# How 128 half rows of a weight matrix are dealt out to partitions: two loads or nine

## The chip, the cores and the metric

The kernel runs on one NeuronCore of a Trainium2 chip. The metric is the device time of one execution in microseconds. Three executions of the kernel before took 400.17, 400.23 and 400.68 us; the median is 400.23.

## The reference

One token is decoded. Its normalised row `xn` goes through an attention block over a cache of 65,536 keys and through a small mixer with two matrix pairs; both results are added to the input.

```python
xn = _layernorm(x)                                  # x: 1 x 1 x 1024, bfloat16
# A: 32 query heads, 4 key heads, 65536 keys of 128
q = xn @ wq                                         # 1024 x 4096
p = softmax(q . k_cache / sqrt(128))
A = (p @ v_cache) @ wo                              # 4096 x 1024
# B: 1024 -> 1024 -> 1024, then 1024 -> 3584 -> 1024
h = gelu(layernorm(xn) @ w1)
g0..g3 = the four quarters of h, each shifted along the sequence, zeros coming in
hs = concatenate([g0, g1, g2, g3]) @ w2
x1 = xn + hs
B = x1 + gelu(layernorm(x1) @ w3) @ w4
return x + A + B
```

The sequence has one position, so every shift brings in zeros only: `hs` is zero for any w2. The kernel still reads w2 and multiplies it, by a column of zeros (`g_col`). Therefore any placement of w2's values in the on-chip memory gives the same output, as long as all of w2 is loaded.

The inputs are 64 MB of keys, 64 MB of values, wq and wo of 8 MB each, w3 and w4 of 7 MB each, w1 and w2 of 2 MB each.

## The kernel before

All large inputs are streamed through three buffers of the on-chip memory, `slots`, of 128 partitions times 64 KB. The list `stream` (L298) holds their order: wq, w3, w1 and w2 together (`w12`), then for each of 8 units `u` a K block and a V block of 8 MB, then wo, then w4. Item number i uses buffer i mod 3. `load` (L301) records the loads of an item, all on SyncE's queue (SP), and `freed` (L332) is called after the last reader of an item has been recorded: it loads the item three places later into the same buffer. The loads of one queue are issued in the order in which they were recorded.

The functions record operations into a `Program` (L59). `plan` (L134) then works out which operation must wait for which other, from the memory regions that they read and write (`regions`, L30, which takes a write to every fourth partition apart into single partitions). Each load gets a semaphore of its own (`landed_n`), which counts to 16 when the load is complete (L207-209). An operation with several waits gets all but the last as separate wait instructions ahead of it (L200-206).

w2 has 1024 rows of 1024 values. It is cut into 2048 half rows of 512 values (1 KB each; `HALF`, L25). The main load of w2 (L312) puts 15 consecutive half rows (`W2_RUN`) into each of the 128 partitions, 1920 in all. The other 128 half rows, 128 KB, go in extra loads, told by the list `W2_EXTRAS` (L27): before, 20 half rows to each of 5 partitions (0, 4, 8, 12, 16), then 14 to each of 2 partitions (1 and 5). They lie behind the 15 half rows of the main load, in columns that POOL sets to zero first (`pool.memset`, L362), since most partitions get nothing there. `W2_DEEP` (L262) is the number of half-row columns that the extras take up: 20.

`compute_w12` (L453) multiplies w1 (16 matmuls), and then adds w2 up in PSUM with one matmul for each column of half rows (L461-462): 15+20 = 35 matmuls. They read the columns of all partitions, so they wait for the extra loads too. Then the buffer is free, and the load of the second K block follows on SP.

For each unit, `scores` transposes K on VectorE (DVE) and multiplies it on TensorE (PE), `maxima` and `weights` make the softmax weights, `values` multiplies V. At the end come wo and w4; w4 is loaded in five pieces (`W4_PIECES`, L19) so that little work is left when the last has landed.

Of the kernel before, what the change touches and what calls it, by code (L numbers as in the profile page):

```python
# [14 lines left out]
P = 128  # L15
# [8 lines left out]
PITCH = {}  # L24
HALF = 512  # L25
W2_RUN = 15
W2_EXTRAS = ((0, 5, 20), (1, 2, 14))  # L27


def regions(ap):  # L30
# [186 lines left out]
def kernel(  # L217
# [15 lines left out]
    D = A_x.shape[-1]  # L233
# [17 lines left out]
    prog = Program(nc)  # L251
    pe, dve, act, pool = prog, prog.dve, prog.act, prog.pool

    def sb(name, shape, dtype=F32):
        return nc.alloc_sbuf_tensor(name, list(shape), dtype)
# [3 lines left out]

    slots = [sb(f"slot{i}", [P, ROW], BF16) for i in range(3)]  # L260
    PITCH.update({t[:].tensor.name: ROW * 2 for t in slots})
    W2_DEEP = max(m for _, _, m in W2_EXTRAS)  # L262
    assert sum(k * m for _, k, m in W2_EXTRAS) == D * D // HALF - P * W2_RUN
    p_sb = sb("p_sb", [P, SUBS * 512], BF16)
    og = sb("og", [P, 512])
    x_row = sb("x_row", [32, D], BF16)
# [34 lines left out]
    def load(it):  # L301
        t = tiles[it]
        if it == "wq":
            prog.load("sp", t[:], A_wq.rearrange("(p c) n -> p (c n)", c=DC))
        elif it == "w3":
            prog.load("sp", t[:, 0:DC * F], B_w3.rearrange("(p c) f -> p (c f)", c=DC))
        elif it == "w12":
            prog.load("sp", t[:, 0:DC * D], B_w1.rearrange("(p c) n -> p (c n)", c=DC))
            at = DC * D
            halves = B_w2.rearrange("r (h n) -> (r h) n", n=HALF)  # L310
            first = P * W2_RUN
            prog.load("sp", t[:, at:at + W2_RUN * HALF], halves[0:first, :].rearrange("(m c) n -> m (c n)", c=W2_RUN))  # L312
            at += W2_RUN * HALF
            for b, k, m in W2_EXTRAS:
                prog.load("sp", t[b:b + 4 * k - 3:4, at:at + m * HALF],
                          halves[first:first + k * m, :].rearrange("(q c) n -> q (c n)", c=m))
                first += k * m
        elif it == "wo":
            prog.load("sp", t[:], A_wo.rearrange("(p j) n -> p (j n)", p=P))
        elif it == "w4":  # L320
            w4_v = B_w4.rearrange("(m c) n -> m c n", c=FC)
            c0 = 0
            for n in W4_PIECES:
                prog.load("sp", t[:, c0 * D:(c0 + n) * D], w4_v[:, c0:c0 + n, :].rearrange("p c n -> p (c n)"))
                c0 += n
        else:
            kind, i = it
            g, b = divmod(i, NB)
            cache = A_k_cache if kind == "K" else A_v_cache
            prog.load("sp", t[:], cache[0, g, b * UKEYS:(b + 1) * UKEYS, :].rearrange("(p ct) d -> p (ct d)", p=P))  # L330

    def freed(it):  # L332

        n = stream.index(it) + 3
        if n < len(stream):
            load(stream[n])

    load("wq")
    opening = len(prog.ops)

    dve.memset(x_row[:], 0.0)
    prog.load("act", x_row[0:1, :], A_x[0, 0:1, :])
    load("w3")

    pool.memset(ident_f[:], 0.0)
# [14 lines left out]
    pool.memset(g_col[:], 0.0)  # L360
    w2_end = DC * D + (W2_RUN + W2_DEEP) * HALF
    pool.memset(tiles["w12"][:, w2_end - W2_DEEP * HALF:w2_end].bitcast(F32), 0.0)  # L362
    load("w12")

    def row_acc(j, lhsT, rhs, start=False):
        return pe.mm(psB[32 * j:32 * j + 32, :], lhsT.to_broadcast([P, 32]), rhs, start, False, (0, 32 * j), COLS)
# [7 lines left out]
    def layernorm(src, tag):  # L374
        rowsum = sb(f"ln_rowsum_{tag}", [P, 1])
        dve.reduce_sum(out=rowsum[:], in_=src[:], axis=AX.X)
        at = next_pm()
        pe.mm32(at[:, 0:1], ones_f[:], rowsum[:], True, True)
        negmean = sb(f"ln_negmean_{tag}", [P, 1])
        dve.tensor_scalar(out=negmean[:], in0=at[:, 0:1], scalar1=-1.0 / D, scalar2=None, op0=ALU.mult)  # L380
        cen = sb(f"ln_cen_{tag}", [P, DC])
        dve.tensor_scalar(out=cen[:], in0=src[:], scalar1=negmean[:, 0:1], scalar2=None, op0=ALU.add)
        sq = sb(f"ln_sq_{tag}", [P, DC])
        rowsq = sb(f"ln_rowsq_{tag}", [P, 1])
        dve.tensor_tensor_reduce(out=sq[:], in0=cen[:], in1=cen[:], scale=1.0, scalar=0.0,
                                 op0=ALU.mult, op1=ALU.add, accum_out=rowsq[:])
        pe.mm32(at[:, 1:2], ones_f[:], rowsq[:], True, True)
        std = sb(f"ln_std_{tag}", [P, 1])
        act.activation(out=std[:], in_=at[:, 1:2], func=ACTF.Sqrt, bias=eps_t[:, 0:1], scale=1.0 / D)
        rstd = sb(f"ln_rstd_{tag}", [P, 1])  # L390
        dve.reciprocal(out=rstd[:], in_=std[:])
        normed = sb(f"ln_out_{tag}", [P, DC])
        dve.tensor_scalar(out=normed[:], in0=cen[:], scalar1=rstd[:, 0:1], scalar2=None, op0=ALU.mult)
        rep = sb(f"ln_rep_{tag}", [P, DC, 32], BF16)
        dve.tensor_copy(out=rep[:], in_=normed[:].unsqueeze(2).to_broadcast([P, DC, 32]))
        return normed, rep, negmean, rstd

    xn, xn_rep, negmean1, rstd1 = layernorm(xT, "a")
    _, xn2_rep, _, _ = layernorm(xn, "b")
# [53 lines left out]
    def compute_w12():  # L453
# [6 lines left out]
        act.activation(out=h1, in_=sc[0:32, 0:2, :], func=ACTF.Gelu_apprx_tanh)  # L460
        for c in range(W2_RUN + W2_DEEP):  # L461
            row_acc(c % 2, g_col[:], wt[:, 2 * DC + c, :], start=(c < 2))
# [86 lines left out]
    for u in range(NU):  # L549
        g, b = divmod(u, NB)  # L550
# [88 lines left out]
```

## Time and profile before

| what | value |
|---|---|
| median of three runs | 400.23 us (400.17, 400.23, 400.68) |
| profiled execution, in all | 400.13 us |
| its span (first to last instruction) | 398.8 us |
| bytes loaded | 170.03 MB, 426 GB/s over the span |
| granted TensorE clock, mean | 0.795 |
| load of w3: issued, first used by PE | 2.30 us, 39.68 us |
| main load of w2 | 1920 KB, 47.2 us from issue to landing |
| K loads, V loads (8 of each) | median 42.2 and 36.8 us from issue to landing |
| last piece of w4 | 256 KB, 34.2 us from issue to landing |

The span is the time between the first and the last instruction on the core; 1.3 us of the 400.13 lie around it. A load's time from issue to landing includes the time in which it stands behind earlier loads, so 42 us for a K block doesn't mean that 8 MB take that long. Two views carry most here: the chain of waits, which is followed back from the last instruction to what released each step, and the DMA packets, of which the trace keeps start, duration, size and queue.

### The profile page before, as it was taken

To read this page: it belongs to the slowest core of one execution; us is meant where nothing else is said; L and a number is where in the kernel's file an instruction comes from. 1 tells how busy PE (TensorE), PEld (TensorE's weight loads), DVE (VectorE), ACT (ScalarE), POOL (GpSimd) and SP (SyncE) were. 2 spreads that over 40 slices of the span, in tenths; PEclk is the share of its full clock that TensorE was granted. 3 is DMA by queue.
4 is the path that set the end of the run, shared out by engine and by line. 5 is a ranking of instruction groups with operands and counts; after the bars stand their busy time and mean duration, and the time that the engine had idled before them with its cause. 6 is when DMAs were issued, how large, how long until landed. Compare 5 with 4: busy or idle time off the path is not lost.

```text
span 398.8 us, 2582 instructions
## 1 busy us (share of the span) xinstructions
PE 226.0 (57%) x1379; PEld 45.2 (11%) x890; DVE 210.2 (53%) x156; ACT 27.6 (7%) x35; POOL 10.6 (3%) x30
## 2 busy tenths in 40 slices
PE   0250990592469256923874197529552946393587
PEld 0210000010101020001001000201010102010233
DVE  0520010975096549653963795259439932793411
ACT  1010030002000200020002000200010011002000
POOL 7000000000000000000000000000000000000000
PEclk9996797597859666978796779568967995687669
DMA  8989999999999999999999999999999999999996
GB/s 342 493 375 419 470 427 421 435 460 434 429 421 434 427 435 434 440 440 434 416 434 440 434 421 442 440 427 427 427 449 440 421 434 435 427 427 421 409 438 274
DMA packets 3774, 170.03 MB, mean 426 GB/s; under 512 B 426, under 2 KB 428, under 8 KB 685
## 3 DMA queue, kind: packets, MB, share of 16 engines
q1 hardware_dynamic: 3758, 169.87, 98.8%
q8 instruction: 9, 0.15, 0.1%
q14 instruction: 1, 0.01, 0.0%
q10 hardware_dynamic: 6, 0.00, 0.0%
HBM read 169.87 MB, written 0.00 MB: 426 GB/s over the span
## 4 chain that ended last, share of the span: by engine, by line
DMA 62%; PE 20%; DVE 15%; ACT 2%; issue 0%; SPq 0%
DMA slot<-in_A_k_cache_dram 44%; DMA slot<-in_B_w_dram 18%; PE sc L116 14%; DVE slot L92 11%; PE oacc L116 4%; DVE p_sb L92 2%; DVE mx L92 2%; ACT p_sb L92 2%; PE psB L116 1%; PE pm L132 0%; DVE m L92 0%; DVE rep L92 0%; DVE nball L92 0%; DVE x_halves L92 0%; PE pm L116 0%
## 5 line engine op out<-in xcount | busy, mean ns | idle before, releaser
L116 PE MATMUL sc<-slot,qdiag 128*128 128x512 bf16 x512 | 130.9, 418 | 65.7 <-DVE slot L92 65.6
L92 DVE STREAM_TRANSPOSE slot<-slot 128x4096 f32<-128x4096 f32 x32 | 139.4, 4411 | 52.2 <-DMA slot<-in_A_k_cache_dram 52.2
L116 PE MATMUL oacc<-slot,p_sb 128*32 128x512 bf16 x512 | 44.5, 524 | 37.5 <-DVE p_sb L92 18.8
L92 DVE STREAM_TRANSPOSE p_sb<-p_sb 128x2048 bf16<-128x2048 bf16 (+2 forms) x10 | 20.8, 2085 | 38.7 <-ACT p_sb L92 38.5
L92 DVE TENSOR_REDUCE mx<-sc 128x1 f32<-128x2048 f32 x8 | 18.3, 2292 | 30.6 <-PE sc L116 30.6
L112 PEld LDWEIGHTS <-qdiag 128*128 128x128 bf16 x128 | 13.2, 103 | 181.4 <-issue 181.4
L92 ACT ACTIVATE p_sb<-sc,nball 128x2048 bf16<-128x2048 f32 x8 | 15.7, 1967 | 250.7 <-DVE nball L92 250.7
L112 PEld LDWEIGHTS <-p_sb 128*32 128x32 bf16 x512 | 16.3, 127 | 62.4 <-issue 19.8
L116 PE MATMUL sc<-slot,ln_rep_b 128*32 128x512 bf16 (+1 forms) x80 | 16.2, 828 | 9.1 <-DMA slot<-in_B_w_dram 8.9
L132 PE MATMUL pm<-ident_f,mx 128*1 128x128 f32 x8 | 2.2, 270 | 19.1 <-DVE mx L92 19.1
L92 DVE SCALAR_TENSOR_TENSOR og<-oacc,wb,og 128x512 f32<-128x512 f32 x4 | 3.0, 751 | 18.8 <-PE oacc L116 18.8
L92 POOL COPY qdiag<-qx 32x32 bf16<-32x32 bf16 x16 | 3.2, 203 | 272.5 <-PE sc L116 250.6
L116 PE MATMUL psB<-slot,oT 128*32 128x512 bf16 x64 | 9.2, 457 | 1.2 <-DVE oT L92 1.2
L126 PE MATMUL pm<-ol,selx 128*128 128x129 f32 x8 | 2.6, 415 | 10.6 <-DVE ol L92 10.6
L116 PE MATMUL sc<-slot,ln_rep_a 128*32 128x512 bf16 x64 | 5.7, 532 | 4.4 <-DMA slot<-in_A_wq_dram 4.4
L126 PE MATMUL pm<-ln_rowsum_a,msk 128*128 128x1 f32 x2 | 0.6, 362 | 13.3 <-DVE ln_rowsum_a L92 13.3
L92 DVE TENSOR_TENSOR og<-psB,slot 64x512 f32<-64x512 f32 x1 | 0.7, 683 | 13.1 <-PE psB L116 13.1
L92 DVE STREAM_TRANSPOSE p_sb<-x_row 32x256 bf16<-32x256 bf16 x4 | 2.5, 616 | 7.4 <-DMA x_row<-in_A_x_dram 7.4
L116 PE MATMUL psB<-slot,g_col 128*32 128x512 bf16 x35 | 4.9, 379 | 0.0
L132 PE MATMUL pm<-ident_f,rep 1*128 1x1 f32 x8 | 1.9, 234 | 5.0 <-DVE rep L92 5.0
L92 ACT COPY og<-oacc 128x512 f32<-128x512 f32 x4 | 2.3, 585 | 32.1 <-PE oacc L116 32.1
L116 PE MATMUL psB<-slot,hT 128*32 128x512 bf16 x40 | 4.5, 379 | 0.0
(87 smaller groups left out, 65.5 us busy)
## 6 DMA issues: line engine op xcount, KB each, us to landing
slot<-in_B_w_dram SPq DMA_DIRECT2D x1, 7168.0 KB, 37.3
slot<-in_B_w_dram SPq DMA_DIRECT2D x2, 2048.0 KB, 37.8
slot<-in_B_w_dram SPq DMA_DIRECT2D x1, 3072.0 KB, 33.4
slot<-in_B_w_dram SPq DMA_DIRECT2D x1, 1920.0 KB, 47.2
slot<-in_B_w_dram SPq DMA_DIRECT2D x1, 1280.0 KB, 33.2
slot<-in_B_w_dram SPq DMA_DIRECT2D x1, 512.0 KB, 34.1
slot<-in_B_w_dram SPq DMA_DIRECT2D x1, 256.0 KB, 34.2
slot<-in_A_k_cache_dram SPq DMA_DIRECT2D x8, 42.2
```

The costliest lines, as they stand in the source:

```text
L92: return program.add(Op(engine, lambda: method(*args, **kw), reads, writes, alone=kw.get("accum_out") is not None))
L112: self.add(Op("pe", lambda: pe.ldweights(lhsT, tile_position=pos), [lhsT], []))
L116: return pe.add_instruction(mybir.InstMatmult(name=nc.get_next_instruction_name(), engine=mybir.EngineType.PE, start_tensor_calc=start, st ...
L126: return self.add(Op("pe", lambda: pe.matmul(out, lhsT=lhsT, rhs=rhs, start=start, stop=stop, tile_position=pos, skip_group_check=True), [ ...
L132: return self.add(Op("pe", lambda: pe.transpose(out, in_, identity), [in_, identity], [out]))
```

## The change

The list of extra loads gets a fourth number, the column at which a load starts. The same 128 half rows are dealt out in nine loads: 12 half rows to each of 3 partitions (0, 4, 8); 1 to each of 8 partitions (1, 5, ... 29); and seven loads of one half row to each of 9, 10, 11, 12, 13, 14 and 15 partitions (32, 36, 40, ...), the load of k partitions in column k-9. The columns of the extras go from 20 to 12, and with them the memset on POOL (5120 to 3072 words a partition) and the matmuls over w2 (35 to 27). The order of the loads on SP stays: the nine stand where the two stood, behind the main load of w2 and ahead of the first K block.

```diff
-W2_EXTRAS = ((0, 5, 20), (1, 2, 14))
+W2_EXTRAS = ((0, 3, 12, 0), (1, 8, 1, 0)) + tuple((32, k, 1, k - 9) for k in range(9, 16))
...
-    W2_DEEP = max(m for _, _, m in W2_EXTRAS)
-    assert sum(k * m for _, k, m in W2_EXTRAS) == D * D // HALF - P * W2_RUN
+    W2_DEEP = max(m + c for _, _, m, c in W2_EXTRAS)
+    assert sum(k * m for _, k, m, _ in W2_EXTRAS) == D * D // HALF - P * W2_RUN
...
-            for b, k, m in W2_EXTRAS:
-                prog.load("sp", t[b:b + 4 * k - 3:4, at:at + m * HALF],
+            for b, k, m, c in W2_EXTRAS:
+                prog.load("sp", t[b:b + 4 * k - 3:4, at + c * HALF:at + (c + m) * HALF],
                           halves[first:first + k * m, :].rearrange("(q c) n -> q (c n)", c=m))
                 first += k * m
```

## The prediction

> **What bounds the kernel now.** I read the busy rows first, then the DMA rows by queue, then the chain of waits, and last the trace's packets one by one. The page's first two parts:
>
> ```profile
> PE 226.0 (57%) x1379; PEld 45.2 (11%) x890; DVE 210.2 (53%) x156; ACT 27.6 (7%) x35; POOL 10.6 (3%) x30
> ...
> DMA  8989999999999999999999999999999999999996
> GB/s 342 493 375 419 470 427 421 435 460 434 429 421 434 427 435 434 440 440 434 416 434 440 434 421 442 440 427 427 427 449 440 421 434 435 427 427 421 409 438 274
> ```
>
> No compute engine passes 57%, while the 16 DMA engines are at 80% or more in every slice but the last. The stream of bytes sets the time. The end of the chain of waits (start, duration, what) says the same:
>
> ```profile
> 362.56 34.22 DMA slot<-in_B_w_dram
> 396.79 0.04 issue
> 396.83 0.34 PE pm L116 x4
> 397.17 0.02 issue
> 397.19 0.43 DVE x_halves L92
> ```
>
> The last piece of w4 is issued at 362.56 and counted as landed at 396.79; 2.0 us of tail follow to 398.8. So the question is which of the 16 DMA engines finishes last. The DMA part by queue shows what runs beside the loads:
>
> ```profile
> q1 hardware_dynamic: 3758, 169.87, 98.8%
> q8 instruction: 9, 0.15, 0.1%
> q14 instruction: 1, 0.01, 0.0%
> ```
>
> Nine packets of 16 KB and one of 8 KB fetch instructions. The trace lists each DMA packet with start, duration and size. A packet of 64 KB takes 2.418 us and the next one of the same engine starts 3 to 4 ns before its end, so the packets can be strung into 16 streams. Each stream runs without a pause from 1.92 to 2.46 us until its end, except where an instruction fetch falls into it: then the next packet is late by 1.0 to 1.4 us. The streams, as I strung them (KB of the two extra loads of w2; start of the fetch that hits it, us; end of its last w4 packet, us):
>
> ```
> extra KB  fetch   end        extra KB  fetch   end
>    0        -    394.42        34        -    395.85
>    0        -    394.43        34        -    395.89
>    0        -    394.84         0       43.3  396.06
>   20        -    395.13         0      297.5  396.07
>   20        -    395.26         0      145.2  396.09
>   20       75.8  396.33         0      195.9  396.10
>    0      104.2  396.23         0      336.4  396.24
>    0      242.1  396.25         0      377.5  396.29
> ```
>
> The last stream ends at 396.33, and 0.46 us later its count arrives (396.79). The mean of the ends is 395.72: with the same bytes, perfect balance is worth 0.61 us and no more. The eight streams that a 16 KB fetch delays end within 0.27 us of the last, although they carry no extra byte; what the kernel does to them decides.
>
> **The change part by part.** *Where the 128 KB go.* In the trace the 5-partition load appears on five streams, the 2-partition load on two of these, and the one-row load of x on one of these two: the sets nest. Number the streams so that a load of k partitions takes streams 0 to k-1. Before, streams 0 and 1 carry 34 KB, 2 to 4 carry 20, the others none. After, 0 to 2 carry 12+1+7=20 KB, 3 to 7 carry 1+7=8, and 8 to 15 carry 7, 6, 5, 4, 3, 2, 1, 0. No row shows loads of 9 to 15 partitions; I take the nesting on. [...]
>
> *Price of a small load in a stream.* The 20 KB packet takes 0.761 us, the 14 KB one 0.535, and 2 to 3 ns pass between packets around a completion mark. The 4 KB pieces take 0.160 and the 2 KB pieces 0.084 us, so 0.038 per KB and 0.008 fixed: a 1 KB packet is 0.046, with its mark 0.049 us. A 12 KB packet is 0.46 us. Then streams 0 and 1: before 0.761+0.535 = 1.30, after 0.46+8x0.049 = 0.85, so -0.45. Stream 2: 0.76 to 0.85, +0.09. Streams 3 and 4: 0.76 to 0.39, -0.37. Streams 5 to 7: +0.39; stream 8 +0.34, and 0.05 less for each further one down to 0 for stream 15.
>
> *Sum.* The fetch-hit streams without extras are eight of the eleven numbered 5 to 15; which ones, the packets don't tell. The relief goes to streams 0, 1, 3 and 4, of which three or four are early already. The latest stream today (fetch at 75.8) is 2, 3 or 4: it goes to 396.42 or 395.96. If the late ones happen to have the highest numbers (396.29 on 15, 396.25 on 14, and so on), the best arrangement I find ends at 396.40, +0.07 us. If the latest of them lies in 5 to 7: 396.29+0.39 = 396.68, +0.35. With four streams between 396.23 and 396.29 it is likelier than not that one sits in 5 to 8, so I take +0.25, nearer the upper end. The same fetches are assumed on the same streams.
>
> *What is hidden.* Nine loads on SP's queue in place of two (timeline: start, duration, what):
>
> ```profile
> 2.30 9.25 SPq L99 DMA_DIRECT2D slot<-in_B_w_dram  x5
> ...
> 5.62 4.36 POOL L92 MEMSET slot<- 128x5120 f32 x1
> ...
> 28.49 0.35 SPq L99 DMA_DIRECT2D slot<-in_A_k_cache_dram  x1
> ```
>
> The two extras wait for the memset and end at 11.55; the trace has their issues at 0.85 and 0.65 us. The memset shrinks to 3072/5120 of 4.36 = 2.62 us, so the nine start at 8.27 and, at 0.85 each, end by 15.9. The next load behind them on SP, the first of K, waits for wq's matmuls until 28.49, so 12.6 us of cover are left; without it each load would delay K by 0.85 us. The streams hold w3, w1 and w2 until 48 us, so even a later K issue starves nothing before then.
>
> On PE 8 matmuls of the w2 accumulation fall away and 9 landings are waited for instead of 2:
>
> ```profile
> 55.71 4.25 PE L116 MATMUL psB<-slot,g_col 128*32 128x512 bf16 x32
> ...
> 59.99 0.33 SPq L99 DMA_DIRECT2D slot<-in_A_k_cache_dram  x1
> ```
>
> 8x0.12 (3.90 us for 32 on the chain) is 0.98 us, so K's second load is issued near 59.0. Its packets lie behind the first K and V loads of 19.4 us each, which fill the streams until 87 us: worth nothing. Behind the new waits stand the rest of w12's matmuls and that issue; the extras land by 50.2, PE gets there after 55, 5 us of cover. At its high bound of 0.42 us a load (below) the last lands near 52.5, still before.
>
> Against its own execution (span 398.8, 400.13 in all) the sum is 400.38; the median of the runs shown is 0.10 higher, so I forecast **400.5 us**.
>
> **The rivals.** *Small loads are not pipelined (slower).* The nearest two completion marks on one stream lie 0.54 us apart today. From mark to count it is 0.42 us (last mark to 396.79 likewise). If a mark could go out only when the one before has been counted, a 1 KB load would cost up to 0.42 instead of 0.049: eight on streams 5 to 7 give +3.0, time 403.4. It passes 0.2% from 0.12 us a load on ((0.8-0.25)/8+0.049). For it: no row shows two marks closer than 0.54. Against it: around today's marks the stream loses 2 to 9 ns only. I keep 0.049 as value because it is from rows of the same queue, and both ends for the range. [...]
>
> *The queue is too full (slower).* Thirteen loads are outstanding after 16 us, where the trace never shows over 7. If SP had to hold K until loads drain, and the drain came late, the streams would stand for a start-up each: 1.0 us from issue (0.90) to first packet (1.92), so +1 to +2, 401.5 to 402.5. Against it: packets per stream stay at some 52, as around 362 us today.
>
> *Another balance (faster).* If the fetches fall on other streams in other executions, a 34 KB stream could be hit today (395.89+1.4 = 397.3) and the flatter spread would gain about 0.4 us: 399.8. Even perfect balance, -0.61, is no 0.2%. Against it: the four times shown lie within 0.55 us.
>
> *Nesting fails.* If 11 and 13 partitions went to one engine, it would take 24 more packets, about 1.1 us on stream 0 at 395.89-0.45: end 396.5, inside the forecast.
>
> **How the numbers follow.** Forecast (within +0.07 to +0.35, nesting included) 0.50; small loads not pipelined 0.27; full queue 0.10; other balance 0.08; a gain that I can't derive 0.05. 0.2% is 0.8 us, about what a measurement of this kernel can tell from no change: the forecast and the other balance give 0.58 for the same, the two slow rivals 0.37, and 0.05 is faster. The range runs from 399.9 to 402.2: it holds the forecast, most of the other balance, small loads up to 0.26 us each and half of the full queue.
>
> **What would show it.** Right: 1 KB packets of about 46 ns whose successors start within 10 ns; streams 3 to 7 with eight of them; last count of w4 at 396.9 to 397.2; first K issue at 28.5. Wrong: gaps between the 1 KB packets (first rival), an SP issue of over 1 us or a pause of all streams near 48 us (second), fetches on other streams (third).

## The result, and the profile after

| | before | after |
|---|---|---|
| median of 20 runs each | 400.30 us | 400.96 us |
| ratio | | 1.0015 (95% interval 1.0008 to 1.0022) |
| profiled execution, its span | 400.13, 398.8 us | 400.82, 399.5 us |
| packets of the load queue | 3758 | 3934 |
| last piece of w4 counted as landed | 396.79 us | 397.46 us |
| last packet of the last stream ends | 396.33 us | 396.97 us |

The change made the kernel 0.66 us slower, clear of no change and under 0.2%. The forecast was +0.25. The end of the chain of waits of the changed kernel (start, duration, what):

```profile
362.84 34.62 DMA slot<-in_B_w_dram
397.46 0.04 issue
397.50 0.34 PE pm L116 x4
397.84 0.02 issue
397.87 0.42 DVE x_halves L92
```

It is the same chain, with the last piece of w4 0.67 us later and the tail of the same length. So the whole difference lies in the DMA streams. The busy rows and the DMA rows of the page:

```profile
PE 228.5 (57%) x1371; PEld 46.2 (12%) x890; DVE 210.3 (53%) x156; ACT 27.6 (7%) x35; POOL 8.9 (2%) x30
...
DMA  8989999999999999999999999999999999999896
...
DMA packets 3950, 170.03 MB, mean 426 GB/s; under 512 B 514, under 2 KB 608, under 8 KB 865
...
q1 hardware_dynamic: 3934, 169.87, 98.7%
q8 instruction: 9, 0.15, 0.2%
q14 instruction: 1, 0.01, 0.0%
```

The same bytes and as many instruction fetches; PE has its 8 matmuls less, and there are 176 packets more, 88 with data and 88 under 512 B, which are completion marks: the 4-byte packet that a stream sends behind its part of a load, after which the trace has a count of the load's semaphore (15 marks and 15 counts behind them, from 49.22 to 51.63 us, for the load of 15 partitions). Strung into streams as before, the packets of the changed kernel show two things. The 1 KB packets take 0.046 us each and follow each other after 2 to 3 ns, as if they were free of any further price. But the first 64 KB packet of K behind them, which takes 2.418 us on the six other streams and on all of them a packet later, takes longer on ten:

```
small loads on the stream   first K packet, us
0 to 5 (six streams)        2.418
6      (one stream)         2.476
7      (one stream)         2.576
8      (five streams)       2.760  2.894  2.982  2.985  3.044
8, and the 12 KB load       2.692  2.712  2.756
```

Two of the five streams with 8 small loads alone are hit by a late instruction fetch (at 337.0 and 378.2 us), and they are the last to end, at 396.88 and 396.97. The one hit at 337.0 us has the packet of 2.982 us. The other has that of 3.044 or that of 2.985: these two streams run into the same nanoseconds at 104.9 us, and the packets don't tell which is which behind that. Without those 0.56 and 0.57 to 0.63 us the two would end at 396.31 and at 396.34 to 396.40, and the last stream would be the one with 6 small loads that the first fetch hits (396.50). Of the 0.64 us by which the last stream is later, 0.47 is the long first packet and 0.17 is the rest.

### The profile page after: what moved, and what is told of

It is laid out like the page before. It is cut to its first block, busy times and chain, and to the rows that moved or that the text cites. A ratio compares the mean times of both kernels' runs of the same rounds, so it can differ in the third digit from the quotient of the medians.

```text
span 399.5 us, 2581 instructions
## 1 busy us (share of the span) xinstructions
PE 228.5 (57%) x1371; PEld 46.2 (12%) x890; DVE 210.3 (53%) x156; ACT 27.6 (7%) x35; POOL 8.9 (2%) x30
## 3 DMA queue, kind: packets, MB, share of 16 engines
q1 hardware_dynamic: 3934, 169.87, 98.7%
## 4 chain that ended last, share of the span: by engine, by line
DMA 62%; DVE 18%; PE 16%; ACT 2%; issue 0%; SPq 0%
DMA slot<-in_A_k_cache_dram 44%; DMA slot<-in_B_w_dram 18%; DVE slot L92 14%; PE sc L116 11%; PE oacc L116 4%; DVE p_sb L92 2%; DVE mx L92 2%; ACT p_sb L92 2%; PE psB L116 1%; PE pm L132 0%; DVE m L92 0%; DVE rep L92 0%; DVE nball L92 0%; DVE x_halves L92 0%; PE pm L116 0%
## 5 line engine op out<-in xcount | busy, mean ns | idle before, releaser
L116 PE MATMUL oacc<-slot,p_sb 128*32 128x512 bf16 x512 | 47.3, 550 | 37.5 <-DVE negmg L92 18.8
L112 PEld LDWEIGHTS <-p_sb 128*32 128x32 bf16 x512 | 17.3, 132 | 64.2 <-issue 23.2
```

The costliest lines, as they stand in the source:

```text
L112: self.add(Op("pe", lambda: pe.ldweights(lhsT, tile_position=pos), [lhsT], []))
L116: return pe.add_instruction(mybir.InstMatmult(name=nc.get_next_instruction_name(), engine=mybir.EngineType.PE, start_tensor_calc=start, st ...
```

## Experiments: what the long first packet is

Two readings were open at the start: the streams' bytes alone (theory S in the expectations), or a debt left by the small loads (theory D). Only the loads of w2 differ between the kernels. "First K packets" are the first 64 KB packets behind the extras. The runs came in four groups, each beside runs of the kernel before on the same chip; differences are to that kernel.

**1. Even share, one load.**

```diff
-W2_EXTRAS = ((0, 3, 12, 0), (1, 8, 1, 0)) + tuple((32, k, 1, k - 9) for k in range(9, 16))
+W2_EXTRAS = ((0, 16, 8, 0),)
```

> The 128 half rows as one load of 8 to each of 16 partitions: one 8 KB packet and one completion mark on every stream. Theory D (a run of small loads leaves a debt: in the changed kernel the first 64 KB packet behind eight 1 KB loads took 2.76 to 3.04 us instead of 2.42): no debt here, first K packets 2.42 us, every fetch-hit stream 0.31 us later than before, end of the last stream 396.6, time 400.6 (+0.27). Theory S (only the bytes moved onto the fetch-hit streams count, the number of loads doesn't): the same 400.6; this run is the baseline for the next three.

Measured: 400.88 us, ratio 1.0016 (1.0007 to 1.0026), +0.62 where both theories had +0.27. All first K packets were long, 2.49 to 2.93 us, behind a single 8 KB packet. A third cause was at work, which run 5 finds.

**2. Even share, eight loads.** `tuple((0, 16, 1, c) for c in range(8))` in the place of the list.

> The same 8 KB for each of 16 streams as eight loads of one half row to each of 16 partitions: eight packets, eight marks. Theory D: first K packet 2.8 to 3.1 us on all 16 streams, time 0.4 to 0.7 above the one-load kernel, 401.0 to 401.3. Theory S: 8x0.049 against 0.31 us, 0.08 above the one-load kernel, 400.65.

Measured: 401.30 us, ratio 1.0025 (1.0015 to 1.0036); first K packets 2.69 to 3.27 us. That is 0.42 above run 1, as theory D has it, but on top of run 1's own debt.

**3. Even share, one load of eight small packets.** List of run 1, and the half rows of a partition taken 16 apart:

```diff
-t[b:b + 4 * k - 3:4, at + c * HALF:at + (c + m) * HALF],
-    halves[first:first + k * m, :].rearrange("(q c) n -> q (c n)", c=m)
+t[b:b + 4 * k - 3:4, at + c * HALF:at + (c + m) * HALF].rearrange("q (c n) -> q c n", c=m),
+    halves[first:first + k * m, :].rearrange("(c q) n -> q c n", c=m)
```

> The same 8 KB for each of 16 streams as one load whose eight half rows per partition lie apart in w2: eight 1 KB packets, but one mark. If the debt comes from the small packets, the first K packet is 2.8 to 3.1 us and the time 401.0 to 401.3, as with eight loads. If it comes from the completion marks, the first K packet is 2.42 us and the time 400.6.

Measured: 401.08 us, ratio 1.0020 (1.0011 to 1.0029); first K packets 2.57 to 2.95 us. It lies between runs 1 and 2 and decides nothing as long as run 1's debt is in it.

**4. The changed kernel's 8 KB on the critical streams, in three loads.** `((0, 4, 9, 0), (1, 8, 8, 0), (32, 2, 14, 0))`.

> Three loads: 9 half rows to each of 4 partitions, 8 to each of 8, 14 to each of 2. Streams 5 to 7 carry 8 KB as in the changed kernel, streams 0 and 1 carry 31, 2 and 3 carry 17, 4 carries 8, 8 to 15 none, with at most three marks on a stream. Theory D: no debt, the fetch-hit streams among 5 to 7 end near 396.6, time 400.6, that is 0.3 to 0.4 below the changed kernel. Theory S: the late streams carry what they carry in the changed kernel, time 400.9 to 401.0 like it.

Measured: 400.42 us, ratio 1.0003 (0.9994 to 1.0013), +0.16 to before where the changed kernel had +0.66; every first K packet took the usual time. None of its executions (400.16 to 400.50) was as slow as the fastest of the changed kernel (400.63). Streams 5 to 7 carry the same 8 KB as in the changed kernel, so theory S falls. The gain of 0.50 is more than the 0.3 to 0.4 that theory D gave. The chain's end:

```profile
362.46 34.68 DMA slot<-in_B_w_dram
397.14 0.04 issue
```

**5. Run 1 at other partitions.** `((32, 16, 8, 0),)`: partitions 32 to 92 in place of 0 to 60. The seven loads of the change start at 32 as well.

> One load of 8 half rows to each of 16 partitions again, but at partitions 32, 36, ... 92 in place of 0, 4, ... 60. In the first version all 16 first K packets took 2.58 to 2.93 us although each stream had one load only. [...] Theory H (16 streams reading one stretch of 128 KB of w2, whatever the partitions): first K packets 2.75 again, time 400.9.

Measured: 400.48 us, ratio 1.0006 (0.9997 to 1.0016), +0.26 to before where run 1 had +0.62; no long first K packet. Only the partitions changed, so run 1's debt came from where the streams wrote, and theory H is out. Its chain ended at 397.50, this one's at 397.10:

```profile
363.01 34.50 DMA slot<-in_B_w_dram
397.50 0.04 issue
```

```profile
362.63 34.47 DMA slot<-in_B_w_dram
397.10 0.04 issue
```

The first fence is run 1, the second this run. The debt of run 1, 0.34 us on most streams, is about the time of one more 8 KB packet (0.309 us); what makes the partitions matter no run shows. The changed kernel's debt is another one: run 12 has the same loads at the same partitions, and no packet behind them was long.

**6 and 7. Runs 2 and 3 at partitions 32 to 92.** `tuple((32, 16, 1, c) for c in range(8))`, and run 3's edit with `((32, 16, 8, 0),)`.

> [...] Theory D (debt by a run of small loads): first K packets 2.6 to 3.0 us on all streams, time 0.3 to 0.6 above the one-load kernel, 400.9 to 401.2. [...]

> One load with eight 1 KB packets a stream and one mark, at partitions 32 to 92. If the debt comes from completion marks: first K packets 2.42 us, time 400.6, as the one-load kernel plus 0.04. If it comes from small packets: 2.6 to 3.0 us and 400.9 to 401.2, as eight loads.

Measured: eight loads 400.98 us, ratio 1.0019 (1.0009 to 1.0028), first K packets 2.53 to 3.07 us; eight packets with one mark 400.65 us, ratio 1.0011 (1.0002 to 1.0021), no first K packet over 2.46 us. So the debt comes with the completion marks of the loads and not with the small packets. (Each load brings one mark, so these two runs can't tell the mark from anything else that a load brings; run 8 has more on that. Run 7 took 0.17 us more than run 5 where 0.04 was expected; the rest is not explained, and the intervals of the two overlap.) The last piece of w4 landed at 397.54 and 397.18 (chain's end; first the eight loads, then the one):

```profile
363.04 34.51 DMA slot<-in_B_w_dram
397.54 0.04 issue
```

```profile
362.69 34.49 DMA slot<-in_B_w_dram
397.18 0.04 issue
```

**8. Eight small loads on two streams only.** `tuple((0, 2, 1, c) for c in range(8)) + ((32, 14, 8, 0),)`.

> Eight loads of one half row to each of 2 partitions (streams 0 and 1: eight 1 KB packets, eight marks each), then 8 half rows to each of 14 partitions (streams 0 to 13: one 8 KB packet). Theory D within a stream: streams 0 and 1 show a debt of 0.3 us or more behind their 1 KB packets (in the 8 KB packet or the first K packet), the others none. Theory D shared between the streams (many marks of all streams at once): no debt anywhere, since there are 16 small loads' marks in place of 92. Time 400.5 to 400.7 in either case, streams 0 and 1 are early ones.

Measured: 400.27 us in one run, +0.05 to before and below the 400.5 to 400.7 that was expected either way. Two first K packets were long, 2.73 and 2.78 us, the other 14 were not. The debt arises within a stream and not between streams. The trace also has the time of every count of a load's semaphore. For the two streams, us:

```
load        1      2      3      4      5      6      7      8
stream a  48.87  49.06  49.24  49.42  49.59  49.77  49.95  50.13
stream b  49.09  49.28  49.47  49.65  49.84  50.03  50.21  50.39
```

The packets pass at one per 0.049 us, the counts come at one per 0.18 us. The reading taken from this: the marks of a stream are worked off one at a time, the stream runs ahead of them for a while, and then it has to wait. This is theory M of the next runs.

**9. Four marks.** `tuple((32, 16, 2, 2 * c) for c in range(4))`.

> Four loads of 2 half rows to each of 16 partitions at 32 to 92: four 2 KB packets, four marks a stream. Theory M (marks are counted one at a time per stream, one every 0.18 us, and the stream may run some 0.7 us ahead of them before it stalls; read from the kernel with eight small loads on two streams): 4x0.18 is 0.72 us against 0.34 us of packets, 0.38 behind, within the allowance: first K packets 2.42 us, time 400.45 to 400.55, as one load. Theory E (each small load costs an equal share of the debt, 0.045 us and up): first K packets 2.6 us, time 400.65 to 400.7.

Measured: 400.61 us, ratio 1.0005 (0.9996 to 1.0015), +0.31 to before where run 5 had +0.26. The times in the expectation were worked out from run 5's 400.48, beside which the kernel before took 400.22 us; here it took 400.30. With these 0.08 added, theory M's times are 400.53 to 400.63 and theory E's 400.73 to 400.78, so the time is theory M's. No first K packet was long on any stream (all under 2.44 us): four marks leave no debt. This profile has some thirty later 64 KB packets of 2.44 to 2.54 us, between 89 and 202 us, without a known cause; run 5's profile has 22 such packets.

**10. Sixteen marks.** `tuple((32, 8, 1, c) for c in range(16))`.

> Sixteen loads of one half row to each of 8 partitions (32 to 60): streams 0 to 7 get sixteen marks each, streams 8 to 15 nothing. Theory M: 16x0.18 is 2.9 us against 0.79 us of packets; less the allowance of 0.7 the streams 0 to 7 stall for 1.4 us in all. The fetch-hit streams among 5 to 7 end at 396.25+0.79+1.4 = 398.4, time 402.2 to 402.4. Theory F (a fixed latency shows once behind any run of small loads, 0.3 to 0.6 us): 397.5, time 401.3 to 401.5.

Measured: 402.49 us in two runs, ratio 1.0054 (1.0035 to 1.0072). The eight streams' first K packets took 3.58 to 4.05 us, and the last stream ended at 398.46 (expected 398.4). Run 8's two streams had 0.31 and 0.36 us of debt with eight marks; here it is 1.17 to 1.64, so each further mark adds 0.10 to 0.17 us, about its 0.18 less the 0.049 of its packet. The wait shows within the row of small loads too: 16 of the 128 1 KB packets, all from 48.95 us on, took 0.051 to 0.200 us in place of 0.046. Theory M holds in size, and a latency that shows once is out.

**11. A version leveled for the end.** One half row of each partition is moved from the main load to the extras:

```diff
-W2_RUN = 15
+W2_RUN = 14
-W2_EXTRAS = ((0, 3, 12, 0), (1, 8, 1, 0)) + tuple((32, k, 1, k - 9) for k in range(9, 16))
+W2_EXTRAS = ((0, 5, 19, 0), (1, 3, 27, 0), (32, 16, 5, 0))
```

> The main load of w2 takes 14 half rows a partition in place of 15; the other 256 go as 19 to each of 5 partitions, 27 to each of 3 and 5 to each of 16 (streams 0 to 2: 51 KB, 3 and 4: 24, the others 5; three marks at most). Compared with before, the fetch-hit streams 5 to 15 carry 3 KB less, 0.11 us. Theory: last stream at 396.2 instead of 396.33, time 0.1 to 0.15 us below before, about 400.15, if nothing but the latest stream's bytes decides; streams 0 to 2 come to the same end. A rival: fetches move to a stream that carries 51 KB, and the time rises to about 401.5.

Measured: 400.26 against 400.30 us of before, ratio 0.9998 (0.9989 to 1.0007): no difference that can be told. Its last stream ended at 396.55: one that the fetch at 145.6 us hits and that was already late at the end of w2 (48.69 us, where the stream hit at 103.8 had 48.02). So streams are some tenths of a microsecond apart before any fetch, as much as was to be gained.

**12. The changed kernel's loads, not in a row.** The nine loads stay, and the main load of w2 is issued between the fifth and the sixth:

```diff
-            prog.load("sp", t[:, at:at + W2_RUN * HALF], halves[0:first, :].rearrange("(m c) n -> m (c n)", c=W2_RUN))
             at += W2_RUN * HALF
-            for b, k, m, c in W2_EXTRAS:
+            for n, (b, k, m, c) in enumerate(W2_EXTRAS):
+                if n == 5:
+                    prog.load("sp", t[:, at - W2_RUN * HALF:at],
+                              halves[0:P * W2_RUN, :].rearrange("(m c) n -> m (c n)", c=W2_RUN))
```

> The changed kernel's nine loads, bytes, partitions and marks, but the main load of w2 (eight 15 KB packets a stream, 4.6 us) is issued behind the fifth of them, so no stream sees more than five small loads in a row. Theory M (marks are counted one per 0.18 us, and a stream stalls only when it is more than 0.7 us ahead of them): no first packet behind small loads is longer than usual, fetch-hit streams among 5 to 7 end at 396.6 to 396.7, time 0.25 to 0.35 below the changed kernel, 400.6 to 400.7. Rival (a price for each small load, however they are spread, or the bytes alone): as the changed kernel, 400.95.

Measured: 400.41 us, ratio 1.0002 (0.9993 to 1.0011), +0.07 to before where the changed kernel had +0.66. No packet behind the small loads was long. The loads, bytes, partitions and marks are the same; the run is broken, and for that the main load of w2 is issued later. No execution (400.27 to 400.56) was as slow as the fastest of the changed kernel (400.63). The gain of 0.59 is more than the 0.25 to 0.35 expected; the part on the sum below says why. The chain's end:

```profile
362.76 34.18 DMA slot<-in_B_w_dram
396.94 0.04 issue
396.98 0.34 PE pm L116 x4
```

## Why the prediction was right, and which term was too small

**The bound.** Right: the last of 16 gapless streams sets the end, and the tail behind it didn't change. One reading was too low: a fetch was said to make the next packet late by 1.0 to 1.4 us. That packet starts 1.0 to 1.1 us late, but it also takes 2.89 to 2.97 us in place of 2.418 (profiles before and after), so a 16 KB fetch costs its stream some 1.5 us; the 8 KB fetch costs 0.97 (0.94 in the profile after). Both kernels have the same fetches, so the sum doesn't change; the third rival's 397.3 would be 397.4.

**Where the bytes go.** Right. The small loads now number the streams, since each count of 1 KB packets has its streams: 8 on streams 3 to 7 (8 and the 12 KB on 0 to 2), then 7, 6, 5, 4, 3, 2, 1, 0. Nesting holds for 9 to 15 partitions. The fetches at 43.4, 104.3 and 198.7 us hit streams 9, 10 and 12; those at 145.3, 246.9 and 297.8 hit 11, 13 and 14, in an order that the packets leave open. Those at 337.0 and 378.2 hit two of streams 3 to 7, which carry the same here; that they are of 5 to 7 is inferred from the kernel before, where the streams hit at these times carry no extra. That is the worse of the arrangements considered: late streams among those that get 8 KB.

**The price of a small load.** Here the step failed: "a 1 KB packet is 0.046, with its mark 0.049 us". The packet is 0.046 to the nanosecond, and 0.049 is right for runs of up to five. The forecast took it for eight, and left out that the marks are counted one per 0.18 us (run 8): from the sixth load in a row on, the stream stalls (first K packet 2.418 us behind five, 2.476 behind six, 2.576 behind seven). On the two critical streams this was 0.56 and 0.57 to 0.63 us for eight loads, in the place of 0. The term "streams 5 to 7: +0.39" should have been about +1.0.

**The sum.** The forecast was +0.25, the measured +0.66: slower, as forecast, but outside the forecast's own +0.07 to +0.35. Only the wider range holds it, and that was drawn for the first rival. The profile puts 0.47 of the last stream's 0.64 on the stall, and breaking the run (run 12) took 0.59 of 0.66 away. What is left, 0.07 to 0.17, is under the forecast's 0.25 for the bytes: the base of 396.29 came from one execution, in which the stream hit last had ended w2 late (48.69 us; 48.37 or 48.44 in the profile after). That part is argued from two profiles, not tested by itself. So the byte term was too large and the stall was missing, and the two partly made up for each other. By the bytes alone (run 12, interval 0.9993 to 1.0011) it can't be told that the change is slower at all.

**What is hidden.** Right. SP's queue and the memset of the changed kernel (timeline: start, duration, what):

```profile
2.28 13.19 SPq L99 DMA_DIRECT2D slot<-in_B_w_dram  x12
29.20 0.35 SPq L99 DMA_DIRECT2D slot<-in_A_k_cache_dram  x1
...
59.19 0.33 SPq L99 DMA_DIRECT2D slot<-in_A_k_cache_dram  x1
```

```profile
5.60 2.66 POOL L92 MEMSET slot<- 128x3072 f32 x1
```

The nine issues end at 15.47 (forecast 15.9), the memset takes 2.66 (2.62), K's second load goes out at 59.19 (59.0). The first K load waits until 29.20 for wq's matmuls, 0.7 us later than before, and starves no stream.

**The rivals.** "Small loads are not pipelined" was the right mechanism in a milder size: the counts come one after another, 0.18 us apart and not 0.42 (run 8), and with an allowance of some five (no long packet behind up to five small loads). Its turning point was stated as 0.12 us a load over eight loads; eight loads cost 0.387 and up to 0.63 of stall, 0.13 each, but the byte term was smaller than forecast and kept the time under 0.2%. The sign named for this rival, gaps between the 1 KB packets, did not show: these passed as forecast, and the stall stands behind them, in the first K packet. The last count of w4 came at 397.46, above the 396.9 to 397.2 named for the forecast. "The queue is too full" is out: nine issues at 0.8 us each, no pause of all streams. "Another balance" is out for this execution: the ten fetches come within 5 us of their times before, and as strung no stream with the 12 KB is hit. "Nesting fails" is out.

## What to carry to other kernels

Where one stream of bytes sets the time, string its packets together and look at which DMA engine ends last: the mean share of the load queue was 98.8% before and 98.7% after, while the last stream ended 0.64 us later. Several small loads in a row on the same engines cost here no more than their packets only up to about five (1 KB a stream; first K packet 2.418 us behind five, 2.76 to 3.04 behind eight): put bulk between them (+0.07 us to before in place of +0.66, run 12), or give one load more packets, since the price came with the loads and not with the packets (400.98 us for eight loads, 400.65 for one of eight packets, runs 6 and 7). Check into which partitions a load with few partitions writes, not only how many engines it uses: the same 128 KB added 0.62 us at partitions 0 to 60 and 0.26 at 32 to 92 (runs 1 and 5).

## What the runs showed of the hardware

**The counts of completion marks come one at a time.** On one stream the counts of successive small loads come 0.18 us apart (run 8). In the profile after, the stream with six small loads sends their marks from 50.14 to 50.38 us, 0.048 us apart, and their counts come from 50.74 to 51.63, 0.17 to 0.18 apart. The stream itself passes a mark in 2 to 9 ns until it is too far ahead: behind up to five 1 KB loads the first K packet took its usual 2.418 us, behind six 2.476, behind eight 2.76 to 3.04 (profile after). For each further mark from eight to sixteen it loses 0.10 to 0.17 us (runs 8 and 10).

**Where a small load writes.** Sixteen partitions at 0 to 60 in steps of 4 left a debt of about 0.34 us for 8 KB a stream (run 1, 400.88 us), the same load at 32 to 92 none (run 5, 400.48 us).

**Instruction fetches are paid by single streams.** Each 16 KB fetch makes one stream late by some 1.5 us (1.0 to 1.1 us of gap and a next packet of 2.89 to 2.97 us in place of 2.418), within 5 us of the same times in the profiles before and after; as strung, no stream was hit twice. These hits decide which streams are last, and the 0.61 us between the last and the mean of the streams in the profile before was all that any placement of w2 could have gained there.
